# A spectrum held in two layouts in one tile, and its transposes as two row tiles of 64

## The chip, the cores and the metric

The kernel runs on one core of a Trainium2 chip. The metric is the device time of one execution in microseconds; the kernel before takes 2072.28 us in the median of three runs (2070.13 to 2073.51). The lower the better.

## The reference, cut to what matters

```python
# x, v: (4, 11456, 128); pos_emb: (11456, 64); w1: (64, 64); w2: (64, 128)
h = np.maximum(pos_emb @ w1, 0) @ w2 * np.exp(-0.01 * pos)[:, None]
u = x * v
L = 2 * S
y = irfft(rfft(u, n=L, axis=1) * rfft(h, n=L, axis=0), n=L, axis=1)[:, :S]
x = (x * y).reshape(45824, 128)
# then a mixture of 8 experts, top 1
logits = x @ w_gate + modality_bias[modality_id]
e = argmax(logits);  gate = softmax(logits)[e]
out = gate * (relu(x @ w1[e]) @ w2[e])          # F = 1024
```

So there is a long convolution along the sequence, for each of 128 features and four batches, and then a routed feed-forward layer over all rows.

## The kernel before, in words

The convolution is a two-step transform over 90 x 64 indices. The kernel calls the index of the first step k1 (N1 = 90 of them) and the 64 places of the second n2; 128 features d are dealt with in 16 groups q of eight.

One large tile `A` of 128 partitions holds the spectrum between the steps. Its partitions are the 64 places n2 in two halves (one for each of two parts `c`), and its free axis is `[2 blocks, 90 k1, 128 d]`. For each batch it is written twice and read twice:

- `transform` in `forward_stages` (L486 to 499): for a group q, 64 matmuls (each shown as two instructions) multiply the products of x and v with `fwd` (90 columns), and two copies on ACT (L498) write A for four features each, all k1: runs of four neighbouring elements, 512 bytes apart.
- `spectrum` in `middle_stages` (L617): for a step g, that is four values of k1, the moving operand of the matmuls L625 is `A[:, :, k1]`, 256 columns, two runs of 128.
- `inverse` (L657): after the products with the filter's spectrum, matmuls L669 transform back, and two copies on ACT (L673) write the same four k1 of A again, 128 neighbouring features at a time.
- `turn` in `inverse_stages` (L690): for a group q and a block, eight PE transposes (L694) take `A[:, blk, :, d]`, 128 partitions by 90 k1 at a step of 512 bytes, as weights, with the 128 x 128 identity as the moving operand. Four of them fill one PSUM bank, and a copy on ACT (L695) takes each of the two banks to a tile `w_t`. Then `transform` of the inverse (L697) multiplies with `inv` (L703), ACT copies one half of the result (L706), and DVE does the rest (L707 to L709).

The work is laid out in stages: a first stage with the filter and the first batch's products, a middle with 23 steps g, an outer stage, a middle, and so on, and a last outer stage that has only the inverse half. An outer stage has 16 indices q. In it the inverse turns of one batch, the routing of its rows (L751 to L838: the row transposes L751 with copies L753, logits, choice of the expert, storing the rows) and the forward products and transforms of the next batch go side by side. The last stage is followed by the experts (L1079 onwards), which the change does not touch.

The order of all of this is written out by hand: each function is put on a time line with an index and an offset (tables OUTER, LAST, MID0 and MID), the events are sorted, and every engine gets its instructions in that order and keeps it. In OUTER a turn of q comes first, then the row transposes, the forward transform of q - 1, and only then the inverse transform L703 of q. In LAST the inverse transform of q comes right after the second turn of q.

PSUM has four single banks (`bank`, used in rotation by the turns, the inverse's matmuls, the row transposes, the logits and the rest) and two pairs of banks (`pair`, used by the forward transform, the inverse transform and the spectrum). A bank is given back when the copy that reads it is done. Three tiles `xo` hold finished rows until they are stored (L809); L709 writes them.

The choice of experts needs two constant matrices `tri` and `ones`, which come as float32 in `small` and are cast to bfloat16 by DVE (L406).

## Time and profile before

| | |
|---|---|
| median of three runs | 2072.28 us |
| profiled execution | 2074.09 us |
| span of its instructions | 2072.3 us |
| mean granted TensorE clock | 0.982 |
| PE busy | 1958.3 us (94%) |
| DVE busy | 1752.4 us (85%) |
| ACT busy | 1284.4 us (62%) |
| POOL busy | 1169.4 us (56%) |
| transposes of the turns, L694 | 1024, 135.5 us |
| their copies, L695 | 256, 133.5 us |
| spectrum matmuls, L625 | 1440, 181.1 us |
| inverse matmuls, L669 | 3576, 228.1 us |
| forward matmuls, L495 | 4096, 100.1 us |

The span runs from the first to the last instruction of one profiled execution; the execution's own time is what lies around that span too. Busy time counts each moment once, so that overlapping matmuls don't count twice; the mean of one instruction does include such overlap. A releaser is what ended an engine's idle time. The clock is a share of full speed, 2.4 GHz. Up to about 1020 us the kernel is in the convolution and the routing, after that in the experts.

### The profile page before, as it was taken

The numbers are of one execution on the slowest core, as the hardware profiler recorded it, in microseconds if no ns is written. First come the engines' busy times: TensorE is split into PE (matmuls) and PEld (weight loads), VectorE is DVE, ScalarE is ACT, GpSimd is POOL, SyncE is SP. The second block draws the span as 40 slices with busy tenths as digits, with TensorE's granted clock in tenths as the row PEclk, the third lists the DMA queues.
The fourth block names the chain that finished last, engine by engine and source line by source line (L and its number), as shares of the span: only waits on it lengthen the run. The fifth ranks groups of instructions, "written<-read, shape, count | busy, mean of one in ns | idle before, by whom it ended". The sixth has DMA issues, their size and how long they took to land. (4 is left out here: it accounts for less than half of the span.)

```text
span 2072.3 us, 50243 instructions
## 1 busy us (share of the span) xinstructions
PE 1958.3 (94%) x17646; PEld 1554.1 (75%) x17646; DVE 1752.4 (85%) x2612; ACT 1284.4 (62%) x2404; POOL 1169.4 (56%) x1054
## 2 busy tenths in 40 slices
PE   8899898999989998999789999999999999999997
PEld 8688665776667665776468888877888888888897
DVE  6599899999999899996678888897888778878886
ACT  5555675457744675456456666666666666666675
POOL 0144004766678476974456678786555555555654
PEclk9999999999999999999899999999999999999998
DMA  8565688889988898856787456654645555555421
GB/s 319 184 191 173 231 280 268 268 264 314 327 270 253 280 339 288 283 183 179 199 248 205 97 127 138 133 124 103 118 97 97 97 100 98 96 98 100 86 40 29
DMA packets 610842, 379.46 MB, mean 183 GB/s; under 512 B 424026, under 2 KB 542005, under 8 KB 610585
## 3 DMA queue, kind: packets, MB, share of 16 engines
q1 hardware_dynamic: 587193, 328.61, 58.2%
q0 software_dynamic: 23104, 47.34, 6.6%
q8 instruction: 141, 2.31, 0.5%
q14 instruction: 116, 0.95, 0.2%
q10 hardware_dynamic: 288, 0.25, 0.1%
HBM read 272.74 MB, written 103.70 MB: 182 GB/s over the span
## 5 line engine op out<-in xcount | busy, mean ns | idle before, releaser
L1094 ACT ACTIVATE hh<-ph 128x512 fp32r<-128x512 f32 x724 | 434.0, 599 | 323.2 <-PE ph L1091 320.2
L1095 DVE SCALAR_TENSOR_TENSOR hl<-ph,hh 128x512 fp32r<-128x512 f32 x724 | 488.5, 680 | 164.4 <-ACT hh L1094 155.6
L276 POOL DMA_INDIRECT xs<-back,to x360 | 405.4, 1126 | 319.9 <-DVE se L797 107.9
L1160 POOL DMA_INDIRECT out<-ot,x x362 | 373.3, 1031 | 160.2 <-issue 36.7
L1089 PE MATMUL ph<-xh,wh 128*128 128x512 f32 (+1 forms) x792 | 298.0, 376 | 8.3 <-ACT wh L1060 8.3
L1091 PE MATMUL ph<-xl,wh 128*128 128x512 f32 (+1 forms) x792 | 296.2, 374 | 9.0 <-POOL xl L1077 9.0
L1115 PE MATMUL po<-hl,wh 128*128 128x512 f32 (+1 forms) x792 | 295.6, 373 | 0.9 <-DVE hl L1095 0.6
L1090 PE MATMUL ph<-xh,wl 128*128 128x512 f32 (+1 forms) x792 | 295.6, 373 | 0.0
L1113 PE MATMUL po<-hh,wh 128*128 128x512 f32 (+1 forms) x792 | 295.1, 373 | 0.2 <-ACT hh L1094 0.2
L1114 PE MATMUL po<-hh,wl 128*128 128x512 f32 (+1 forms) x792 | 294.7, 372 | 0.0
L673 ACT COPY A<-pw 128x512 f32<-128x512 f32 (+1 forms) x184 | 97.1, 580 | 188.1 <-PE pw L669 188.1
L1077 POOL TENSOR_TENSOR xl<-xT,xh 128x512 fp32r<-128x512 f32 (+1 forms) x77 | 96.2, 1250 | 203.2 <-ACT xh L1073 203.2
L669 PEld LDWEIGHTS pw<-work 64*128 64x128 f32 x2856 | 167.2, 189 | 32.1 <-ACT work L607 19.2
L625 PE MATMUL pz<-A,work 128*64 128x256 f32 x1440 | 181.1, 394 | 8.3 <-DMA work<-in_c_to 5.0
L638 POOL TENSOR_TENSOR work<-work 128x512 f32<-128x512 f32 (+1 forms) x92 | 115.3, 1253 | 129.0 <-DVE work L634 128.4
L669 PE MATMUL pw<-work 64*128 64x128 f32 x2856 | 181.6, 279 | 4.7 <-POOL work L655 4.3
L1091 PEld LDWEIGHTS ph<-xl,wh 128*128 128x128 f32 x792 | 150.5, 190 | 37.0 <-POOL xl L1077 10.8
L1089 PEld LDWEIGHTS ph<-xh,wh 128*128 128x128 f32 x792 | 150.5, 190 | 33.6 <-ACT wh L1060 8.5
L1115 PEld LDWEIGHTS po<-hl,wh 128*128 128x128 f32 x792 | 150.0, 189 | 29.8 <-DVE hl L1095 4.2
L1090 PEld LDWEIGHTS ph<-xh,wl 128*128 128x128 f32 x792 | 150.6, 190 | 26.1 <-DVE wl L1061 0.4
L1113 PEld LDWEIGHTS po<-hh,wh 128*128 128x128 f32 x792 | 150.0, 189 | 26.1 <-ACT hh L1094 0.7
L1114 PEld LDWEIGHTS po<-hh,wl 128*128 128x128 f32 x792 | 150.0, 189 | 25.7
(181 smaller groups left out, 3613.9 us busy)
## 6 DMA issues: line engine op xcount, KB each, us to landing
work<-hs SPq DMA_DIRECT2D x66, 512.0 KB
work<-in_x SPq DMA_DIRECT2D x64, 512.0 KB
work<-in_xd SPq DMA_DIRECT2D x58, 512.0 KB
work<-in_v SPq DMA_DIRECT2D x51, 512.0 KB
xr<-xo SPq DMA_DIRECT2D x64, 365.6 KB
back<-xr SPq DMA_DIRECT2D x120, 195.0 KB
work<-in_c_to SPq DMA_DIRECT2D x88, 256.0 KB
blocks<-xs SPq DMA_DIRECT2D x328, 64.0 KB
```

Source lines behind the costliest of these rows:

```text
L276: s = pool.indirect_dma_start(out=xs, out_offset=bass.IndirectOffsetOnAxis(ap=ix, axis=0), in_=src, in_offset=None, bounds_check=E * R - 1 ...
L625: pe.matmul(z[64 * s:64 * s + 64, t, r], k["b"][:, t, s, r], A[:, :, 4 * g + 2 * t + s], start=True, stop=True)
L669: pe.matmul(v[s][:, t, blk], k[of][at, t, r, blk], k["c"][at, t, r], start=i == 0, stop=i == len(terms) - 1)
L1089: pe.matmul(p, k[0, "h"][:, f:f + D], k["xh"], start=True, stop=False)
L1090: pe.matmul(p, k[0, "l"][:, f:f + D], k["xh"], start=False, stop=False)
L1091: pe.matmul(p, k[0, "h"][:, f:f + D], k["xl"], start=False, stop=True)
L1094: act.activation(hh, ph, AF.Relu)
L1095: steps.append(ins_of(dve.scalar_tensor_tensor(hl, ph, 0.0, hh.bitcast(F32), op0=ALU.max, op1=ALU.subtract)))
L1113: pe.matmul(po, k[1, "h"][:, f], hh[:, t], start=g == 0, stop=False)
L1114: pe.matmul(po, k[1, "l"][:, f], hh[:, t], start=False, stop=False)
L1115: pe.matmul(po, k[1, "h"][:, f], hl[:, t], start=False, stop=g == NCH - 1)
L1160: s = pool.indirect_dma_start(out=out, out_offset=bass.IndirectOffsetOnAxis(ap=ix, axis=0), in_=src, in_offset=None, bounds_check=N - 1, o ...
```

## The change

The tile A is laid out anew, as `[32 groups, 736]`, where a group is a block and eight features, and the 90 k1 are padded to KP = 92. Two views of the same words are used in turn. `A_fwd` has in each group first k1 mod 4, then k1 div 4, then the eight features: the forward copies write fours of features, 32 bytes apart, and the spectrum reads 32 rows of eight. `A_inv` has in each group four pairs, and for each pair all k1 with the two features of the pair side by side: the inverse's copies write pairs, and the turns read 90 k1 at a step of 8 bytes. A step g of the middle reads and writes the same words in both views.

A turn is now 16 transposes instead of eight: each takes 64 partitions and a 64 x 64 part of the identity, and the two halves of the partitions go to two banks `p[0]` and `p[1]`. Both banks are taken at the start, and each of the two copies takes one bank, that is one half of the rows for all eight features, to blocks of 64 in `w_t`.

`fwd` has 92 columns, two of them zero. The matrices `tri` and `ones` come as bfloat16 inside `small`, so the cast goes. The tiles mx, mb and se of the choice have one buffer instead of two.

```diff
@@ -37,6 +37,7 @@
 N = B * S
 NP = N1 // 2
 NM = (NP + 1) // 2
+KP = 4 * NM
 NQ = N2 // 4
 NO = N2 // 8
 NC = 16
@@ -98,8 +99,8 @@
     turn = 2 * np.pi / (8 * N1)
     phi = turn * (((4 * k1[None, :] + 1) * (2 * n1[:, None] + 1)) % (8 * N1))
     even, odd = np.cos(phi) + np.sin(phi), np.cos(phi) - np.sin(phi)
-    fwd = np.zeros((2, 64, 2, N1))
-    fwd[:, :HALF, 0], fwd[:, :HALF, 1] = even, odd
+    fwd = np.zeros((2, 64, 2, KP))
+    fwd[:, :HALF, 0, :N1], fwd[:, :HALF, 1, :N1] = even, odd
     whole = np.zeros((2, 64, 2, N1))
     whole[:, :HALF, 0], whole[0, :HALF, 1], whole[1, :HALF, 1] = even, odd, -odd
     inv = np.zeros((N1, 2, 64))
@@ -131,7 +132,8 @@
     keep = np.ones((D, E, NC))
     keep[:, :, 0] = 0
     q, p = np.arange(D)[:, None], np.arange(D)[None, :]
-    tri = np.concatenate([-(q >= p).astype(float), np.ones((D, D))], 1)
+    tri = np.concatenate([-(q >= p).astype(np.float32), np.ones((D, D), np.float32)], 1)
+    tri = np.ascontiguousarray(tri.view(np.uint32) >> 16).astype(np.uint16).view(np.float32)
     small = np.concatenate([
         order(tok)[:, 0:NC],
         first.reshape(D, E * NC), keep.reshape(D, E * NC), tri,
@@ -142,7 +144,7 @@
     pad[:, :, D + 1] = np.array(NOWHERE, np.int32).view(np.float32)
     f = lambda a: np.ascontiguousarray(a, dtype=np.float32)
     return {
-        "c_fwd": f(fwd.reshape(D, 2 * N1)), 
+        "c_fwd": f(fwd.reshape(D, 2 * KP)), 
         "c_inv": f(inv.reshape(N1, D)), "c_to": f(to), "c_back": f(back), "c_early": f(np.concatenate([win.reshape(D, 2 * N2), whole.reshape(D, 2 * N1)], 1)),
         "c_small": f(small), "c_pad": f(pad.reshape(D, -1)),
     }
@@ -173,7 +175,7 @@
 SMALL = {}
 _at = 0
 for _name, _n in (("tok", NC), ("first", E * NC), ("keep", E * NC),
-                  ("tri", D), ("ones", D), ("reg", E), ("iota", NF)):
+                  ("both", D), ("reg", E), ("iota", NF)):
     SMALL[_name] = (_at, _at + _n)
     _at += _n
 NSMALL = _at
@@ -212,7 +214,7 @@
     warm = cst.tile([1, 2], F32, name="warm")
     dve.memset(warm, 0.0)
 
-    both = cst.tile([D, 2 * D], BF16, name="both")
+    both = sm("both").bitcast(BF16)
     tri, ones = both[:, 0:D], both[:, D:2 * D]
     base = cst.tile([D, E], F32, name="base")
     base1 = cst.tile([D, E], F32, name="base1")
@@ -375,8 +377,10 @@
             return pairs.tile([D, 2, 512], F32, tag="pp", name=name)
 
         work = keepp.tile([D, 17 * U + 4 * PU], F32, name="work")
-        A = keepp.tile([D, 2, N1, D], F32, name="A")
-        fwd = keepp.tile([D, 2, N1], F32, name="fwd")
+        A = keepp.tile([D, 2 * NQ, 8 * KP], F32, name="A")
+        A_fwd = A.rearrange("p (b q) (j g n) -> p b q j g n", b=2, j=4, n=8)
+        A_inv = A.rearrange("p (b q) (h k i) -> p b (q h) k i", b=2, h=4, i=2)
+        fwd = keepp.tile([D, 2, KP], F32, name="fwd")
         inv = keepp.tile([N1, 2, 64], F32, name="inv")
         bs2 = keepp.tile([D, NO, E, NC], F32, name="bs2")
         early = bs2.rearrange("p o e c -> p (o e c)")[:, 0:2 * N2 + 2 * N1]
@@ -403,7 +407,6 @@
 
         def split_constants():
             dve.tensor_scalar_add(base, sm("reg"), FAR)
-            dve.tensor_copy(both, small[:, SMALL["tri"][0]:SMALL["ones"][1]])
 
         pool.memset(wg, 0.0)
 
@@ -420,7 +423,7 @@
 
         flat = lambda t: t.rearrange("p a b c r -> p (a b c r)")
         spans = back.rearrange("p k c r -> p (k c r)")
-        flatA = A.rearrange("p b k d -> p (b k d)")
+        flatA = A.rearrange("p c r -> p (c r)")
         for name, of in (
                 ("emb", [flatA[:, (16 + i) * U // 2:(17 + i) * U // 2] for i in range(NQ)]),
                 ("c0", [spans[:, i * U // 2:(i + 1) * U // 2] for i in range(3)]),
@@ -492,11 +495,10 @@
                         for c in range(2):
                             for blk in range(2):
                                 at = slice(64 * blk, 64 * blk + 64)
-                                pe.matmul(p[64 * c:64 * c + 64, blk, N1 * j:N1 * j + N1],
+                                pe.matmul(p[64 * c:64 * c + 64, blk, KP * j:KP * j + KP],
                                           e[at, c, 4 * h + j], fwd[at, c], start=True, stop=True)
-                    d0 = 8 * q + 4 * h
-                    act.copy(A[:, :, :, d0:d0 + 4],
-                             p[:, :, 0:4 * N1].rearrange("p b (n k) -> p b k n", n=4))
+                    act.copy(A_fwd[:, :, q, :, :, 4 * h:4 * h + 4],
+                             p[:, :, 0:4 * KP].rearrange("p b (n g j) -> p b j g n", n=4, j=4))
 
             return load, product, transform
 
@@ -623,7 +625,7 @@
                     for r in range(2):
                         for s in range(2):
                             pe.matmul(z[64 * s:64 * s + 64, t, r], k["b"][:, t, s, r],
-                                      A[:, :, 4 * g + 2 * t + s], start=True, stop=True)
+                                      A_fwd[:, :, :, 2 * t + s, g], start=True, stop=True)
                 k["pz"] = pz[:, 0:n].rearrange("p t (r b d) -> p (t r) b d", r=2, b=2)
 
             def products(g):
@@ -670,8 +672,8 @@
                                           start=i == 0, stop=i == len(terms) - 1)
                 for s in range(2):
                     k1 = 4 * g + s
-                    act.copy(A[:, :, k1:k1 + 2 * n - 1:2].rearrange("p b t m -> p t b m"),
-                             v[s][:, 0:n])
+                    act.copy(A_inv[:, :, :, k1:k1 + 2 * n - 1:2].rearrange("p b m t i -> p t (b m) i"),
+                             v[s][:, 0:n].rearrange("p t b (m i) -> p t (b m) i", i=2))
 
             todo = dict(inverse=inverse, spectrum=spectrum, products=products, load_c=load_c,
                         load=load, swap=swap)
@@ -688,11 +690,15 @@
                 sp.dma_start(t, a["x"][b, q])
 
             def turn(q, blk):
+                p = [bank("wt")[0:N1].rearrange("p (c j n) -> p c j n", c=2, j=4) for _ in range(2)]
                 for c in range(2):
-                    p = bank("wt")
                     for j in range(4):
-                        pe.transpose(p[0:N1, D * j:D * j + D], A[:, blk, :, 8 * q + 2 * j + c], ident)
-                    act.copy(w_t[q % 2][blk][:, c], p[0:N1])
+                        for t in range(2):
+                            at = slice(64 * t, 64 * t + 64)
+                            pe.transpose(p[t][:, c, j], A_inv[at, blk, 4 * q + j, 0:N1, c], ident[at, at])
+                w = w_t[q % 2][blk].rearrange("p c (j t n) -> p t c j n", j=4, t=2)
+                for t in range(2):
+                    act.copy(w[:, t], p[t])
 
             def transform(q):
 
@@ -776,7 +782,7 @@
                 i = b * NO + o
                 xo = xo_of(b, o)
                 lg = kept.pop(o)
-                mx = rt.tile([PU, NC], F32, tag="mx", name="mx")
+                mx = rt.tile([PU, NC], F32, tag="mx", name="mx", bufs=1)
                 dve.tensor_reduce(mx, ec(lg), axis=AX.X, op=ALU.max)
                 dl = lg
                 dve.tensor_sub(dl, lg, wide(mx))
@@ -785,14 +791,14 @@
                 oh, sc = oh_t[i % 2], sc_t[i % 2]
                 sco = rt.tile([PU, E, NC], F32, tag="sco", name="sco", bufs=1)
                 dve.scalar_tensor_tensor(sco, dl, 0.0, fst, op0=ALU.is_ge, op1=ALU.mult)
-                mb = rt.tile([PU, NC], F32, tag="mb", name="mb")
+                mb = rt.tile([PU, NC], F32, tag="mb", name="mb", bufs=1)
                 dve.tensor_reduce(mb, ec(sco), axis=AX.X, op=ALU.max)
                 dve.scalar_tensor_tensor(oh[0:PU], sco, 0.5, wide(mb), op0=ALU.max,
                                          op1=ALU.is_equal)
                 dve.tensor_tensor_scan(
                     sc[0:PU].rearrange("p e c -> p (e c)"), sm("keep")[0:PU],
                     oh[0:PU].rearrange("p e c -> p (e c)"), 0.0, op0=ALU.mult, op1=ALU.add)
-                se = rt.tile([PU, NC], F32, tag="se", name="se")
+                se = rt.tile([PU, NC], F32, tag="se", name="se", bufs=1)
                 dve.tensor_reduce(se, ec(ex), axis=AX.X, op=ALU.add)
                 dve.tensor_scalar_add(se, se, 1e-9)
                 xov = xo[0:PU].rearrange("p w s h r -> p h (w s) r")
```

## Rows read from the trace of the kernel before

**Rows 1.** the page's part 1: busy us (share of the span) xinstructions

```profile
PE 1958.3 (94%) x17646; PEld 1554.1 (75%) x17646; DVE 1752.4 (85%) x2612; ACT 1284.4 (62%) x2404; POOL 1169.4 (56%) x1054
```

**Rows 2.** stretches: us; busy of PE, PEld, DVE, ACT, POOL; clock, DMA, GB/s

```profile
96.00:208.00 112.00, 111.44 (x1388) 91.17 (x1384) 102.08 (x98) 63.20 (x132) 49.15 (x39) 1.00 0.57 180
240.00:330.00 90.00, 86.84 (x1325) 59.97 (x1324) 85.16 (x157) 68.69 (x134) 3.31 (x4) 1.00 0.78 265
```

**Rows 3.** timeline of PE, 228 to 241 us: start, us, engine, line, operation

```profile
230.49 1.94 PE L703 MATMUL py<-work,inv 90*64 90x512 f32 x8
...
232.35 2.01 PE L694 MATMUL wt<-ident,A 128*90 128x128 f32 x16
...
236.77 1.94 PE L703 MATMUL py<-work,inv 90*64 90x512 f32 x8 [0.26 <-ACT A L498]
```

**Rows 4.** timeline of ACT, 230 to 241 us

```profile
232.47 0.59 ACT L706 COPY work<-py 128x512 f32<-128x512 f32 x1 [1.10 <-PE py L703]
233.14 2.06 ACT L695 COPY work<-wt 90x512 f32<-90x512 f32 x4
...
235.96 1.42 ACT L498 COPY A<-s 128x720 f32<-128x720 f32 x2
```

**Rows 5.** waits of DVE, 225 to 800 us: total us, times, longest

```profile
DVE work L707 <- ACT work L706: 18.2, 16, 3.2
```

**Rows 6.** timeline of PE, 916 to 945 us

```profile
922.50 2.00 PE L694 MATMUL wt<-ident,A 128*90 128x128 f32 x16
924.43 2.36 PE L703 MATMUL py<-work,inv 90*64 90x512 f32 x8
926.72 1.14 PE L694 MATMUL wt<-ident,A 128*90 128x128 f32 x8
```

**Rows 7.** timeline of ACT, 916 to 945 us

```profile
923.23 2.06 ACT L695 COPY work<-wt 90x512 f32<-90x512 f32 x4
```

**Rows 8.** timeline of DVE, 984 to 1012 us

```profile
988.45 0.25 DVE L802 RECIPROCAL xo<-se 109x16 f32<-109x16 f32 x1
...
997.09 1.23 DVE L709 TENSOR_TENSOR xo<-work 128x1024 f32<-128x1024 f32 x1 [2.82 <-DMA xr<-xo]
```

**Rows 9.** groups by line and form: xcount, busy us, mean ns, idle before

```profile
L669 PE MATMUL pw<-work 64*128 64x128 f32 x2856 | 181.6, 279 | 4.7 <-POOL work L655 4.3 <-DVE work L655 0.3
...
L625 PE MATMUL pz<-A,work 128*64 128x256 f32 x1440 | 181.1, 394 | 8.3 <-DMA work<-in_c_to 5.0 <-DVE work L643 2.3 <-ACT A L498 0.9
...
L694 PE MATMUL wt<-ident,A 128*90 128x128 f32 x1024 | 135.5, 283 | 2.9 <-ACT A L673 2.9
L695 ACT COPY work<-wt 90x512 f32<-90x512 f32 x256 | 133.5, 600 | 10.3 <-PE wt L694 7.1 <-ACT work L761 0.2 <-issue 0.2
...
L673 ACT COPY A<-pw 128x512 f32<-128x512 f32 x176 | 94.5, 589 | 185.2 <-PE pw L669 185.2
...
L498 ACT COPY A<-s 128x720 f32<-128x720 f32 x128 | 92.0, 762 | 21.5 <-PE s L495 20.8
...
L495 PE MATMUL s<-fwd,work 64*64 64x90 f32 x3264 | 77.6, 242 | 6.1 <-DVE work L708 4.1 <-issue 1.5 <-ACT A L498 0.4
...
L526 ACT ACTIVATE A<-m,bs 128x64 f32<-128x64 f32 x32 | 7.2, 387 | 13.1 <-PE m L515 13.1
...
L673 ACT COPY A<-pw 128x256 f32<-128x256 f32 x8 | 2.6, 375 | 2.8 <-PE pw L669 2.8
```

**Rows 10.** lines L495, L669, L694, weight loads: ns min/median/max, first and last start

```profile
L495 PEld LDWEIGHTS s<-fwd,work x3264: 129/133/223, 60.3 to 798.0; 64*64 64x64 f32 x192
...
L669 PEld LDWEIGHTS pw<-work x2856: 182/188/334, 351.4 to 917.1; 64*128 64x128 f32 x191
...
L694 PEld LDWEIGHTS wt<-ident,A x1024: 177/180/216, 220.9 to 1007.7; 128*90 128x90 f32 x171
```

**Rows 11.** timeline of all engines, 587 to 600 us

```profile
592.11 1.95 PE L625 MATMUL pz<-A,work 128*64 128x256 f32 x16
...
593.98 2.95 PE L669 MATMUL pw<-work 64*128 64x128 f32 x48
```

## The prediction, made before the changed kernel was run

> **What bounds the kernel now.** The first part of the page [rows 1] is read first: PE is busy 94% of the span, DVE 85%, ACT 62%. From that alone any PE time that is taken away would seem to be time won. The next view is the table of stretches [rows 2], because the change touches only the outer stages and the four middles between them, and these have different limits. The middle of the first row leaves PE 0.56 us of 112 idle: there a slower matmul costs its full time. The outer stage of 240 to 330 us has PE at 86.84 of 90 and DVE at 85.16 of 90, both nearly full, so that the busy shares don't tell which of them ends a step.
>
> So the chain inside an outer stage has to be followed. Early in each stage it is this [rows 3, 4]: L703 starts on PE at 230.49, its result is copied by ACT (L706) at 232.47, then ACT runs the four copies of the turns (L695, from 233.14), two of the rows' turn and the first spectrum copy (L498, 235.96), and L703 of the next index starts at 236.77, when that copy has given back its pair of banks (the mark "0.26 <-ACT A L498"). The steps are 1.98 + 0.67 + 2.82 + 0.81 = 6.28 us, the whole period. The loop goes over ACT, which has no idle mark from L706 on, and PE has 0.26 us to spare in it. Later in the stage DVE sets the pace: in 225 to 800 us, three outer stages and the two middles between them, it waited for L706 16 times and 18.2 us in all [rows 5]. That 18.2 us is the most that a faster turn can give back there.
>
> The last stage has two phases. First it is paced by the turn, its copies and L703, 926.72 - 922.50 = 4.2 us per index until other work joins it [rows 6]. Towards its end a loop without PE sets the pace [rows 8]: the choice ends with L802 at 988.45, its rows are stored, and the next L709 has waited 2.82 us for such a store when it starts at 997.09.
>
> **The change part by part.**
>
> *Turn, on PE.* A turn is now 8 transposes of 128 rows; after, 16 of 64 rows with 64 streamed columns, in two row tiles. Two turns take 924.43 - 922.50 = 1.93 us from start to start [rows 6], so one takes 0.965 us. No row shows a transpose in two row tiles. The nearest is L669, 64 rows in two row tiles with 128 weight columns and 128 streamed ones: 181.6 us for 2856, 63.6 ns each [rows 9]. Taken whole it gives 16 x 63.6 = 1.02 us, 0.05 more than now; scaled by streamed columns (64/128) 0.51 us, 0.46 less. I take it scaled by weight columns (90/128): 45 ns, 0.72 us, 0.25 less, because with only 64 streamed columns the load should be the longer part. Over 128 turns that is 31 us of PE work less (7 more to 58 less).
>
> *Turn, on ACT.* The same two copies of 512 elements (600 ns [rows 9]), but each now holds one half of the rows for all eight indices, so both wait for the end of the turn. Today the first copy starts 923.23 - 922.50 = 0.73 us after the turn begins [rows 6, 7]: 0.48 us for four transposes and 0.25 us on the way. After the change it starts at 15/16 of 0.72 + 0.25 = 0.93 us. In the loop of rows 3 and 4 the copies begin 233.14 - 232.35 = 0.79 us after the turn does, so the loop grows by 0.14 us although PE does less. About ten indices of the three stages are in that phase (16 waits, some of them in the phase that DVE sets): +1.4 us. What PE saves there becomes idle time before L703.
>
> *Last stage.* L703's second matmul reads the second block, and now needs both copies of it instead of the first alone. Four copies take 2.06 us [rows 7]; the last ends at 922.50 + 0.93 + 2.06 = 925.49. L703 then has three quarters of its 1.86 us (232.35 - 230.49) to go and ends at 926.9 against 926.72 if its two column tiles overlap again at once, at 927.2 if the first of the three runs alone. I take +0.35 us; six indices before the store's loop takes over: +2.0 us. In that loop a turn that is a few tenths later costs nothing; without slack the other ten indices would cost 3.5 us more, which I keep for the range, as I keep zero for the first six.
>
> *Forward transform.* 92 streamed columns for 90. The largest group of L495 has 3264 instructions in 77.6 us [rows 9], so all 4096 (64 per index) make 97 us; 2.2% is 2.1 us of PE, of which a quarter, the first stage's share, lies on the path: +0.5 us. Its copy has 736 elements instead of 720: 13 ns at the rate that L498 and L673 show between them, (762 - 589)/208 = 0.83 ns per element, inside the rounding of the 1.4.
>
> *Inverse's copies (L673).* They write runs of two elements instead of 128. Runs of four cost nothing: L498 already writes fours, and L673's 375 ns for 256 and 589 for 512 put 720 at 763; it took 762. Single elements do cost something: L526, 64 of them at a step of 256 bytes, took 387 ns where the same line gives 215; 2.7 ns for each, unless its scale operand has a part in it [rows 9]. So pairs lie between 0 and 256 x 1.67 = 427 ns more per copy, the upper end if a run of two takes as long as a run of four. I take 0, since the nearest row with runs is free. The upper end is a rival below. The Trainium skill's "SBUF — State Buffer" (SBUF: two separate sides, on cachelines of 16 bytes) says that two hits on a line are enough for full bandwidth; by it the pairs are free and the sum stays, and the upper end would add the rival's 12 us. No run here shows it for ACT.
>
> *Spectrum's reads (L625).* 256 columns in 32 rows of eight instead of two of 128. No moving operand of this size in the trace has steps. The nearest row is a weight load of this same tile: 90 columns at 512 bytes took 180 ns, where 64 and 128 adjacent ones took 133 and 188, so 155 for 90 [rows 10]: 25 ns for 90 hops, 0.28 ns per hop. For 32 hops in one instruction that is 9 ns, for 1440 instructions 13 us; nothing below zero, since these reads are contiguous now. I take 0: seven of eight reads stay adjacent.
>
> *The rest.* One DVE cast goes, estimated from the small DVE operations around L802 (0.25 us [rows 8]) at -0.3 us. The tiles mx, mb and se keep one buffer; DVE alone writes and reads them, in order, so nothing waits. No DMA is added or moved past another on SP's or POOL's queue.
>
> Sum: +1.4 + 2.0 + 0.5 - 0.3 = +3.6 us. The profiled execution took 2074.09 us with a span of 2072.3, 1.8 us above the median of the runs, 2072.28; the difference is put on the median: 2075.9 us. 0.2%, 4.1 us, is about what a measurement of this kernel can tell from no change, so this is a forecast of no measurable change that leans to slower.
>
> **The rivals.**
>
> *The turn is on the path after all.* DVE's 16 waits in the outer stages [rows 5] end with the ACT copy behind L703, PE is 96% busy there [rows 2], and the last stage has six indices that the turn paces. If the ACT copies pack closer than I think, each of the 22 shrinks by what a turn saves on PE, 22 x 0.25 to 22 x 0.46, 5.5 to 10 us. Against it stands ACT's loop without a gap [rows 4]. Time: 2064.
>
> *Slower, the reads of rows of eight.* In the middles PE runs L625 and L669 back to back (592.11 + 1.87 = 593.98 [rows 11]), so every ns per L625 is paid. At the 9 ns above: 13 us, 2085. It decides from 3 ns per instruction (4.1 us / 1440). For it: strided weights do load slower. Against: seven of eight reads stay adjacent.
>
> *Slower, pairs on ACT.* At 427 ns the two copies of a step take 0.85 us longer, and the swap's copies behind them, for which DVE waits in the first middle, come later. ACT is busy 63.20 us of 112 there [rows 2], so I let half of it through: 23 steps x 0.43 make 10 us; the other middles add 2: 2084.
>
> *The middle loses its overlap.* Both layouts lie over the same words. If a step's spectrum had to wait for the copies of an earlier step's inverse, PE would stand for two copies of 589 ns and the 0.25 us on the way, 1.4 us in each of 92 steps, 130 us. For it: the patterns of all steps interleave through the whole tile. Against it: a step reads and writes the same words, other steps others, and today's patterns interleave too without such a wait in the group's row of L625 [rows 9]. 2206 at worst.
>
> **How the numbers follow.** Forecast 0.48 (own range 2072 to 2080), turn on the path 0.27, reads 0.10, pairs 0.10, overlap lost 0.05. Faster by over 0.2%: 0.26 of the second and 0.02 of the first, 0.28. Slower: 0.14 of the first and 0.24 of the last three, 0.38. The same: the rest, 0.34. The range 2062 to 2092 takes in the second case (5.5 to 10 us), the bounds of reads and pairs, and leaves out lost overlap and reads at several times 9 ns.
>
> **What would show it.** L694 should have 2048 instructions and less busy time than its 135.5 us, with L625's mean still near 394 ns and L673's near 589. The loop of rows 4 should be 0.1 to 0.2 us longer with more idle time before L703, and the waits of L707 for L706 as long as now or longer. Wrong: L694's group above 150 us, L625 above 400 ns, L673 above 650 ns, L707's waits down by over 5 us, or a wait of L625 for L673.

## The result, and the profile after

The changed kernel takes 2099.49 us in the median of four runs (2092.9 to 2101.9), the kernel before 2072.78 us beside it: a ratio of 1.0132, 95% interval 1.0118 to 1.0146, so 1.3% slower. 2075.9 us had been forecast, 24 us less, and the measured time lies outside the range. The profiled execution took 2099.63 us with a span of 2097.9.

The first part of the page after, against [rows 1]:

```profile
PE 1962.9 (94%) x18670; PEld 1531.0 (73%) x18670; DVE 1750.9 (83%) x2611; ACT 1301.9 (62%) x2404; POOL 1156.5 (55%) x1054
```

The groups of the lines that the change touches (busy us, mean ns, idle time before), against [rows 9]. L698, L701, L627, L675 and L500 are the former L694, L695, L625, L673 and L498:

```profile
L627 PE MATMUL pz<-A,work 128*64 128x256 f32 x1440 | 182.3, 396 | 8.8 <-DVE work L645 5.6 <-DMA work<-in_c_to 1.2 <-DVE work L636 1.1
...
L701 ACT COPY work<-wt 90x512 f32<-90x512 f32 x256 | 145.5, 582 | 35.4 <-PE wt L698 31.3
...
L698 PE MATMUL wt<-ident,A 64*90 64x64 f32 x2048 | 111.4, 249 | 13.8 <-ACT work L701 9.1 <-ACT A L675 3.0
...
L675 ACT COPY A<-pw 128x512 f32<-128x512 f32 x176 | 103.8, 650 | 179.9 <-PE pw L671 179.9
...
L500 ACT COPY A<-s 128x736 f32<-128x736 f32 x128 | 94.1, 782 | 18.9 <-PE s L498 18.4 <-DMA xo<-in_v 0.2
```

The transposes did get shorter: 111.4 us for 135.5. The spectrum's reads of rows of eight cost nothing (396 ns for 394). The writes of pairs cost 61 ns each (650 for 589). And ACT is now idle for 35.4 us before the turns' copies, where it was 10.3.

The middles did not move (first to last spectrum matmul 126.3, 106.1, 104.0 and 108.4 us before; 127.0, 103.7, 106.3 and 108.4 after). The time went into the stages with turns. From the first to the last L713 (the former L707) the three outer stages take 108.2, 108.1 and 108.2 us for 103.0, 104.0 and 105.6, and the last stage 101.0 for 90.2: 5.2 + 4.1 + 2.6 + 10.8 = 22.7 of the 25.6 us by which the span grew. The rest lies ahead of the first turn (1.9) and in the experts (1.7), about what these parts differ by between kernels that share their code: the first L713 came between 226.9 and 231.7 us in the runs below.

**An outer stage.** PE of the kernel before, in its first outer stage, over one whole period of two indices. One of them has the logits (L759) and is called the long index here, the other the short one:

```profile
258.80 0.94 PE L759 MATMUL pl<-work,wg 128*32 128x436 f32 x8
...
264.95 1.94 PE L703 MATMUL py<-work,inv 90*64 90x512 f32 x8 [0.26 <-ACT A L498]
266.82 2.00 PE L694 MATMUL wt<-ident,A 128*90 128x128 f32 x16
268.66 0.91 PE L751 MATMUL xT<-ident,xo 109*128 109x109 f32 x8
269.51 1.49 PE L495 MATMUL s<-fwd,work 64*64 64x90 f32 x64
271.24 1.94 PE L703 MATMUL py<-work,inv 90*64 90x512 f32 x8 [0.23 <-ACT A L498]
273.10 0.94 PE L759 MATMUL pl<-work,wg 128*32 128x436 f32 x8
```

and of the changed kernel, the same stretch of work:

```profile
261.93 0.94 PE L765 MATMUL pl<-work,wg 128*32 128x436 f32 x8
...
263.03 0.97 PE L698 MATMUL wt<-ident,A 64*90 64x64 f32 x17
264.58 0.89 PE L698 MATMUL wt<-ident,A 64*90 64x64 f32 x15 [0.59 <-ACT work L701]
...
268.52 1.94 PE L709 MATMUL py<-work,inv 90*64 90x512 f32 x8 [0.26 <-ACT A L500]
270.39 1.56 PE L698 MATMUL wt<-ident,A 64*90 64x64 f32 x32
271.94 1.21 PE L757 MATMUL xT<-ident,xo 109*128 109x109 f32 x8
273.08 1.50 PE L498 MATMUL s<-fwd,work 64*64 64x92 f32 x64
275.17 1.94 PE L709 MATMUL py<-work,inv 90*64 90x512 f32 x8 [0.59 <-ACT A L500]
277.04 0.94 PE L765 MATMUL pl<-work,wg 128*32 128x436 f32 x8
```

The period was 273.10 - 258.80 = 14.30 us and is 277.04 - 261.93 = 15.11. In the kernel before PE has only two small gaps (0.26 and 0.23) in it, both for ACT's copy: the loop of PE and ACT was itself 14.3 us long. DVE's loop was level with it. In the next period of the kernel before, where DVE has no idle mark at all, its L707 stands

```profile
273.84 0.70 DVE L707 TENSOR_TENSOR work<-py,work 128x512 f32<-128x512 f32 x1
...
288.15 0.69 DVE L707 TENSOR_TENSOR work<-py,work 128x512 f32<-128x512 f32 x1
```

that is 14.31 us from one to the next but one. The short index grew from 271.24 - 264.95 = 6.29 to 275.17 - 268.52 = 6.65 us, although its two turns shrank from 1.84 to 1.55: L757 takes 0.3 longer and L709 waits 0.59 for 0.23. The long one, the rest of the period, grew from 8.01 to 8.46: its second turn stops after one transpose and waits 0.59 us for a bank, because a turn now takes both of its banks at once.

ACT of the changed kernel in the short index, against [rows 4]:

```profile
270.51 0.59 ACT L712 COPY work<-py 128x512 f32<-128x512 f32 x1 [0.43 <-PE py L709]
271.31 2.29 ACT L701 COPY work<-wt 90x512 f32<-90x512 f32 x4 [0.21 <-PE wt L698]
273.50 0.94 ACT L759 COPY work<-xT 128x436 f32<-128x436 f32 x2
274.33 1.47 ACT L500 COPY A<-s 128x736 f32<-128x736 f32 x2
```

1.99 + 0.80 + 3.02 + 0.84 = 6.65 us. The second term grew by 0.13 (0.67 before): the copies start late, 0.92 us after the turn. The third grew by 0.20 (2.82 before): four copies take 2.29 us for 2.06. Both copies of a turn write interleaved blocks of 64 in one region of `w_t`, and the second carries a wait for the first, which it did not have.

DVE's waits, of the changed kernel from 225 to 810 us, against [rows 5], then in the last stage (920 to 1020 us):

```profile
DVE work L713 <- ACT work L712: 32.7, 27, 2.3
...
DVE work L713 <- ACT work L712: 25.4, 13, 3.9
DVE ro L831 <- PE pr L829: 4.9, 4, 1.2
```

The kernel before in its last stage (920 to 1020 us):

```profile
DVE work L707 <- ACT work L706: 12.3, 10, 2.7
DVE xo L709 <- DMA xr<-xo: 12.2, 5, 3.0
```

**The last stage.** The waits for stores are gone, and those for ACT have doubled: the loop over the turns paces the whole stage. Its PE, against [rows 6], first at the start, then at two later indices:

```profile
930.78 1.56 PE L698 MATMUL wt<-ident,A 64*90 64x64 f32 x32 [0.76 <-ACT A L675]
932.96 3.03 PE L709 MATMUL py<-work,inv 90*64 90x512 f32 x8 [0.61 <-ACT work L701]
935.91 1.56 PE L698 MATMUL wt<-ident,A 64*90 64x64 f32 x32
...
1016.48 0.88 PE L698 MATMUL wt<-ident,A 64*90 64x64 f32 x16
...
1019.88 1.07 PE L709 MATMUL py<-work,inv 90*64 90x512 f32 x2
1021.16 1.93 PE L709 MATMUL py<-work,inv 90*64 90x512 f32 x6 [0.21 <-ACT work L701]
...
1030.43 0.88 PE L698 MATMUL wt<-ident,A 64*90 64x64 f32 x16
```

An index is 935.91 - 930.78 = 5.13 us instead of 4.22, and a later pair 1030.43 - 1016.48 = 13.95 us, where L707 came 8.63 + 4.25 = 12.88 us apart in the kernel before. In LAST the inverse matmul follows the second turn at once, so that PE stands while ACT copies (the marks of 0.61 and 0.21).

### The profile page after: what moved, and what is told of

Its sections match the earlier page's. It is cut to its first block, busy times and chain, and to the rows that moved or that the text cites. A ratio compares the mean times of both kernels' runs of the same rounds, so it can differ in the third digit from the quotient of the medians.

```text
span 2097.9 us, 52014 instructions
## 1 busy us (share of the span) xinstructions
PE 1962.9 (94%) x18670; PEld 1531.0 (73%) x18670; DVE 1750.9 (83%) x2611; ACT 1301.9 (62%) x2404; POOL 1156.5 (55%) x1054
## 5 line engine op out<-in xcount | busy, mean ns | idle before, releaser
L278 POOL DMA_INDIRECT xs<-back,to x360 | 392.9, 1091 | 358.0 <-DVE sc L798 112.0
L675 ACT COPY A<-pw 128x512 f32<-128x512 f32 (+1 forms) x184 | 106.5, 639 | 181.6 <-PE pw L671 181.6
L627 PE MATMUL pz<-A,work 128*64 128x256 f32 x1440 | 182.3, 396 | 8.8 <-DVE work L645 5.6
L1120 PEld LDWEIGHTS po<-hh,wl 128*128 128x128 f32 x792 | 149.9, 189 | 25.6
```

The source lines that it names most:

```text
L278: s = pool.indirect_dma_start(out=xs, out_offset=bass.IndirectOffsetOnAxis(ap=ix, axis=0), in_=src, in_offset=None, bounds_check=E * R - 1 ...
L627: pe.matmul(z[64 * s:64 * s + 64, t, r], k["b"][:, t, s, r], A_fwd[:, :, :, 2 * t + s, g], start=True, stop=True)
L1120: pe.matmul(po, k[1, "l"][:, f], hh[:, t], start=False, stop=False)
```

## Experiments

Four kernels at a time ran beside the kernel before, on four chips. Chip 1: the layout, the turn, late copies, halves in runs of 64. Chip 2: the change again, the second copy's wait, halves in runs of 256, the new LAST. Chip 3: the other orders. Chip 4: the change once more and the three that mix the turns. The kernel before took 2111 us on chips 1 and 2, 2070 and 2072 on 3 and 4. So ratios are compared, and beside them the spacing of L713 in the first outer stage, which was the same to 0.01 us in all three profiles of the change (9.13 + 5.98 = 15.11 a pair). The length of a whole stage is compared only between kernels on chips of the same kind: on chip 1 the outers of the layout alone, which is level with the kernel before, took 109.0, 111.9 and 113.3 us.

**The layout with the old turn.** The turn of the kernel before, from `A_inv`:

```diff
-                        for t in range(2):
-                            at = slice(64 * t, 64 * t + 64)
-                            pe.transpose(p[t][:, c, j], A_inv[at, blk, 4 * q + j, 0:N1, c], ident[at, at])
...
+                        pe.transpose(p[0:N1, D * j:D * j + D], A_inv[:, blk, 4 * q + j, 0:N1, c], ident)
+                    act.copy(w_t[q % 2][blk][:, c], p[0:N1])
```

> The changed kernel with the turn of before: eight transposes of 128 rows, one bank and one copy for each parity of the feature, read from the new layout at a step of 8 bytes. Theory (the turn's way to its copies costs the 27 us: both copies begin only after the whole turn and come 0.57 to 0.60 us apart instead of 0.48): about 2075 us, that is before plus the 1.7 us by which the first stage grew; the copies of the turn are 0.48 us apart and the last stage takes 111 us from its first turn to the experts' first matmul, as before, not 122.7. Rival A (the layout costs: pair writes of 650 ns for 589, first copies of 782 for 762, 92 columns): 2094 to 2100, since nothing of that is undone.

Measured 1.0015 (0.9997 to 1.0034), pairs of 14.30 us. The layout, and with it the 92 columns of `fwd`, the constants and the tiles with one buffer, costs nothing that can be told, although the inverse's copies took 650 ns here too. It even shortens the weight load of a turn:

```profile
L696 PE MATMUL wt<-ident,A 128*90 128x128 f32 x1024 | 131.9, 279 | 5.4 <-ACT A L675 3.0 <-issue 2.2
L696 PEld LDWEIGHTS wt<-ident,A 128*90 128x90 f32 x1024 | 114.4, 163 | 44.2 <-issue 25.3 <-PE py L705 7.3 <-DVE sco L789 4.1
```

163 ns a load in the mean at a step of 8 bytes; at 512 the mean was 183 (median 180, [rows 10]).

**The turn with the old layout.**

```diff
-                        pe.transpose(p[0:N1, D * j:D * j + D], A[:, blk, :, 8 * q + 2 * j + c], ident)
...
+                        for t in range(2):
+                            at = slice(64 * t, 64 * t + 64)
+                            pe.transpose(p[t][:, c, j], A[at, blk, :, 8 * q + 2 * j + c], ident[at, at])
...
```

> The kernel before with the new turn alone: 16 transposes of 64 rows in two row tiles, read from the old layout at a step of 512 bytes. Theory: 2094 to 2099 us, with copies of the turn 0.57 to 0.60 us apart, the loop of an outer stage at 6.6 us for 6.28 and the last stage at 122 us. Rival A (the layout): 2072 to 2076. Besides: if the step of the weights matters for row tiles, two turns take clearly more than the 1.55 us of the changed kernel; else the same.

Measured 1.0188 (1.0154 to 1.0221), pairs of 9.39 + 6.17 = 15.56 us. The turn alone carries the loss. Without the layout it gains nothing on PE:

```profile
L696 PE MATMUL wt<-ident,A 64*90 64x64 f32 x2048 | 131.6, 269 | 17.5 <-ACT work L699 8.5 <-issue 4.0 <-ACT A L673 3.3
L696 PEld LDWEIGHTS wt<-ident,A 64*90 64x90 f32 x2048 | 116.8, 209 | 61.1 <-issue 34.3 <-ACT work L699 11.6 <-DVE mb L793 5.7
```

**Late copies alone.** The kernel before, its transposes of 128 rows filling both banks in turn, so that both copies start late and neither waits for the other:

```diff
+    p = [bank("wt") for _ in range(2)]
+    for j in range(4):
+        for c in range(2):
+            pe.transpose(p[c][0:N1, D * j:D * j + D], A[:, blk, :, 8 * q + 2 * j + c], ident)
```

> The kernel before, with the eight transposes of a turn in another order: the two parities alternate, so that both banks are full only at the end and both copies start late, as in the changed kernel, but 128 rows, old layout, copies 0.48 us apart. First copy at 7/8 of 0.965 + 0.25 = 1.09 us after the turn's start, later than the changed kernel's 0.92. If the late start alone makes the cost: 2090 us or more. If, as I think, the closer pace of the copies keeps the outer stages under DVE's 14.3 us for two indices (6.28 + 0.3 and some 7.3 + 0.3 us), only the last stage and the first indices pay: 2076 to 2082.

Measured 1.0089 (1.0060 to 1.0119), more than the 4 to 10 us expected; pairs of 9.16 + 6.31 = 15.47 us. Late copies and two banks at once are enough to lengthen the pair by more than the change does (15.11), without row tiles and without a wait between copies. The copies here start even later than the change's, 1.12 us after the turn for 0.92, so the run shows what such a delay does and not how much of the change's loss it is. In the last stage the delay costs 7.0 us (96.5, and 89.5 with the layout alone on the same chip), less than the change's 10.8. The late start and the taking of both banks are not told apart by any run; what each does is read from the traces alone.

**The second copy's wait alone.** The kernel before, a bank holding both `c` of two pairs of indices: copies as early as before, but to interleaved parts of `w_t`:

```diff
+    for h in range(2):
+        p = bank("wt")[0:N1].rearrange("p (c r) -> p c r", c=2)
...
+        act.copy(w_t[q % 2][blk][:, :, 2 * D * h:2 * D * h + 2 * D], p)
```

> The kernel before, with its turns of 128 rows and its early copies, but a bank holds both c of two index pairs, so that the two copies of a turn write to interleaved parts of w_t and the second waits for the first; nothing else. Theory (the wait costs only where the loop has no slack): copies come 0.57 instead of 0.48 us apart, the loop of two indices grows by 0.4 to about 14.0 us and stays under DVE's 14.3, the last stage grows by about 3: ratio 1.0015 (1.000 to 1.003). Rival (the wait is the main cost of the change): 1.008 or more.

Measured 1.0039 (1.0021 to 1.0057), over what I expected. On PE:

```profile
264.63 1.94 PE L705 MATMUL py<-work,inv 90*64 90x512 f32 x8 [0.26 <-ACT A L498]
...
271.12 1.94 PE L705 MATMUL py<-work,inv 90*64 90x512 f32 x8 [0.47 <-ACT A L498]
```

The short index is 6.49 us for 6.29, 0.20 us more; four copies take 2.33 us here for 2.06. The pair is 9.17 + 5.56 = 14.73. The slack of 0.3 us that I still supposed is not there; a longer loop lengthens the pair at once.

**The change without that wait.** First with each copy in a half of its own and the inverse matmul reading runs of 64, then with runs of 256 and the order put right in L712 to L714:

```diff
-    act.copy(w[:, t], p[t])
+    act.copy(w_t[q % 2][blk][:, t], p[t].rearrange("p c j n -> p (c j n)"))
...
+    w_t[q % 2][blk].rearrange("p t (c r) -> p c t r", c=2)[:, c]   # 2nd version; 1st: "p t (c j n) -> p c j t n"
```

> The changed kernel, but each half's copy goes to 512 words of its own instead of every other block of 64, and the inverse matmuls read the two halves in rows of 64; the second copy then need not wait for the first to finish. Theory: the four copies of an index come 0.48 us apart, 0.2 to 0.3 us sooner in all, the outer loop falls from 6.65 to about 6.4 us and two indices to below DVE's 14.3, which gives back 8 to 10 us there and some 4 us in the last stage: about 2086 us. Rival B (the late start and the two banks at once are all of it, the pace of the copies nothing): 2096 to 2100.

> The changed kernel, but each copy of a turn fills a half of w_t of its own (row tile t, then c, j, n), the inverse matmul reads two runs of 256, and the order of columns is put right in the ACT copy and the two DVE additions behind it (runs of 64). The second copy no longer overlaps the first's region. Theory (late start and the second copy's wait for the first together push the PE and ACT loop past DVE's 14.3 us for two indices): four copies in 2.06 us instead of 2.29, the short index of an outer stage from 6.65 to about 6.45 us, two indices from 14.33 to about 13.9, which DVE then covers, so the three outers lose most of their 3 to 4 us each, and the last stage about 3 of its 11: ratio 1.007 (1.004 to 1.009). Rival (the late start alone does it, the wait is free): 1.013 as the change. Rival (the wait alone does it): 1.000 to 1.003. Runs of 64 on DVE could cost: then its additions take over 0.69 us.

> The changed kernel once more, unaltered, as the measure for the runs beside it. Every theory expects its first ratio to the kernel before, 1.013 (1.012 to 1.015).

Measured 1.0228 (1.0187 to 1.0269) and 1.0217 (1.0196 to 1.0238). The change itself, beside the second of them, gave 1.0227 (1.0176 to 1.0279) instead of the 1.013 I expected: no gain could be seen there, and one under 0.5% could not have been. The reads in runs of 64 were not to blame: eight inverse matmuls still took 1.94 us in the first outer stage. PE in the second version:

```profile
265.81 1.94 PE L708 MATMUL py<-work,inv 90*64 90x512 f32 x8 [0.26 <-ACT A L500]
...
272.27 1.94 PE L708 MATMUL py<-work,inv 90*64 90x512 f32 x8 [0.47 <-ACT A L500]
```

and its ACT, in the second outer stage:

```profile
476.21 2.04 ACT L700 COPY work<-wt 90x512 f32<-90x512 f32 x4 [0.27 <-PE wt L698]
```

Four copies in 2.04 us, the short index at 6.46. But the long index still waits for a bank (0.64 us), and the pair is 14.97 for 15.11. I had taken DVE to cover all above that; it does not.

What made the change lose 1% more on these chips sits mainly in the last stage. Against the layout alone on chip 1, the change's outers on chip 2 (112.2, 117.1 and 118.1 us) are 13.2 us longer in sum, close to the 11.9 of the first comparison; but its last stage of 115.0 us is 25.5 longer, where the first comparison gave 10.8. In it the granted clock fell (it is the third column from the end; the last row lies mostly at the lower of the two levels, 1.2 GHz):

```profile
980.00:1000.00 20.00, 17.83 (x155) 9.42 (x153) 11.73 (x23) 11.42 (x23) 6.80 (x7) 1.00 0.46 133
1000.00:1020.00 20.00, 19.82 (x129) 9.74 (x126) 9.49 (x24) 8.75 (x19) 5.82 (x6) 0.58 0.61 158
```

Two inverse transforms (L709) in that stretch took 4.59 and 4.93 us on PE, where they take about 3.0 at the full clock. Ahead of it PE stood for copies at every index (17.83 us busy of 20). In the first profile of the change, with the clock at 1.00 from 960 to 1040 us, the stage took 101.0. The clock fell in the last stage of both runs of halves as well (118.5 and 117.9 us), but not with the turn in the old layout on chip 1 (107.6 us), where PE waits too. Why it fell there and not elsewhere stays open.

**Where the loss sits.** The old turn in the last stage alone, and in the outers alone:

```diff
+    turn = turn_128 if b == nb - 1 else turn_64      # outers only; the other run has them exchanged
```

> The changed kernel, unaltered, as the whole to which the two halves beside it are added: 1.013 on a chip where the kernel before takes some 2072 us, 1.023 where it takes some 2111.

> The changed kernel, with the turns of 128 rows and early copies in the last stage alone; the three outer stages keep the two row tiles. Theory (two places of loss that add: 5 us in each outer, by 0.8 us a pair of indices, and 11 us in the last stage): the last stage is that of before, the outers those of the change: ratio 1.007 (1.005 to 1.009) on the faster kind of chip. Rival (it is one loss, and stages downstream pass it on): near 1.013 or near 1.000.

> The reverse: row tiles in the last stage alone, turns of 128 rows and early copies in the outers. Theory: pairs of 14.3 us in the outers, the last stage 101 us as in the change: ratio 1.006 (1.004 to 1.008); its excess and that of the run with row tiles in the outers alone add to the change's within 0.002.

Measured 1.0118 (1.0093 to 1.0144) for the change, 1.0064 (1.0044 to 1.0085) for the outers alone, 1.0051 (1.0035 to 1.0068) for the last stage alone: 0.64% + 0.51% = 1.15%. Two losses that add. The spacing says the same: 108.2, 108.2, 108.2 and 89.8 us with row tiles in the outers; 103.5, 103.6, 104.6 and 101.0 with them in the last stage.

**The order of the stages.** In the last stage both turns behind the inverse, in the outers the row transposes behind the forward transform:

```diff
-LAST = ("inverse:1 logits:3 turn0:0 half:2 lturn:3 turn1:0 ...
+LAST = ("inverse:1 turn0:0 turn1:0 logits:3 half:2 lturn:3 ...
...
-OUTER = ("turn0:0 turn1:0 lturn:3 biased:3 half:2 product:0 forward:1 ...
+OUTER = ("turn0:0 turn1:0 lturn:3 biased:3 product:0 forward:1 half:2 ...
```

> The changed kernel, with the order of the last stage's table altered alone: inverse, turn0, turn1, logits, half, lturn instead of inverse, logits, turn0, half, lturn, turn1, so that a turn's copies are not followed at once by the matmuls that read them. Theory (in the last stage the copies stand bare between the second turn and the inverse matmul, 0.6 us of wait at each index and more): the stage falls from 101.8 us to 88 to 93, the kernel to 1.007 (1.005 to 1.009) of before, 9 to 13 us under the change. Rival (the last stage is paced by its stores or by the routing's DVE chain, and the copies only show there): no change, 1.013. Rival (the logits then come late and lturn waits): up to 1.016.

> The changed kernel with the outer stages' table altered alone: half (the transposes of rows and their copies on ACT) behind forward instead of ahead of it. Theory (the late copies push the row copies and the forward copies of ACT back, and the inverse matmul waits 0.6 us for a buffer that the first forward copy has to empty): the forward copy now stands 0.95 us earlier on ACT, that wait goes, the pair of indices in the first outer falls from 15.11 us to 14.3 to 14.6, some 8 to 15 us less over three outers: ratio 1.006 to 1.010 on a chip where the change is 1.013, 1.015 to 1.020 where it is 1.023. Rival (the time is in the turns themselves, the second of which waits for a bank): pairs stay at 15.1, no change. The last stage stays as in the change under both.

> The changed kernel with both orders: half behind forward in the outers, and in the last stage both turns behind the inverse, ahead of logits and half. Theory: both places of the loss are closed, the outers at DVE's 14.3 to 14.6 a pair, the last stage as before: ratio 1.002 (0.999 to 1.006). Rival (the late start costs in any order): 1.008 or more.

> As the run with both orders, and the two copies of a turn in separate halves of w_t, so that the second does not wait for the first (copies 0.48 us apart again). Theory: 0.1 us a turn less on ACT, worth something only if ACT still paces: ratio 0 to 0.002 under the run with both orders, 1.001 (0.998 to 1.005); under 1.000 it would beat the kernel before. Rival: the same as with both orders.

> The kernel before with the same two orders, nothing of the change. Theory (its outers are paced by DVE's 14.30 us a pair and its last stage by DVE and the stores, so that the order of PE and ACT is free): 1.000 (0.998 to 1.003). Rival (the orders are better in themselves): 0.995 or less; then what the orders win in the changed kernel is no mending of the change.

> Row tiles in the last stage alone, and there with both turns behind the inverse, ahead of logits and half. Theory (both places of loss closed, one by the old turn and one by the order; PE paces neither stage): 1.000 (0.998 to 1.003). Rival (PE's 0.2 us a turn is worth something where the last stage is busiest on PE): 0.998 or less, and this version would beat both.

Measured: LAST alone 1.0115 (1.0097 to 1.0134) beside a change of 1.0227, its last stage 92.3 us for 115.0 (part of that is the clock above; on chip 3, with it at 1.00 in both down to the stage's end, the new LAST made 91.9 of 101.0). OUTER alone 1.0090 (1.0056 to 1.0125); pairs of 9.13 + 5.79 = 14.92 us, not the 14.3 to 14.6 expected. Both 1.0064 (1.0047 to 1.0082), both with separate halves 1.0045 (1.0028 to 1.0062), not told apart from each other; outers of 105.2 to 105.9 us, last stages of 91.9 and 90.5. The kernel before with both orders 1.0026 (1.0012 to 1.0039). Row tiles in the last stage alone, with the new LAST, 1.0014 (0.9999 to 1.0029).

The new LAST gives back nearly all of the last stage (91.9 us, and 90.2 in the kernel before). There the stores are waited for again; DVE's waits with both orders, from 925 to 1010 us:

```profile
DVE work L713 <- ACT work L712: 15.0, 9, 2.7
DVE xo L715 <- DMA xr<-xo: 8.6, 4, 2.5
```

The new OUTER frees L709 from its wait but has one of its own. PE of the run with it alone:

```profile
268.63 0.86 PE L498 MATMUL s<-fwd,work 64*64 64x92 f32 x32
270.21 0.86 PE L498 MATMUL s<-fwd,work 64*64 64x92 f32 x32 [0.71 <-DVE work L714]
...
271.90 1.94 PE L709 MATMUL py<-work,inv 90*64 90x512 f32 x8
```

The forward's second pair of banks is the one that DVE reads the last inverse from. So the order has a floor of 14.92 to 15.0 us whatever the turn is; the kernel before rises to 9.21 + 5.78 with it. In the profiled executions the outers with this order take 106.1 to 106.4 us without row tiles, so that in it row tiles no longer lengthen them. No version here is faster than the kernel before.

## Why the prediction was wrong, point by point

- *Turn, on PE*: right. Two turns take 1.55 us from start to start, 48 ns a transpose (45 forecast), 24 us of busy time less (31 forecast). Scaling by weight columns fits: between the two layouts the row tiles' group and its mean weight load change by the same factor (131.6/111.4 = 209/177 = 1.18). For 128 rows they do not (135.5/131.9 = 1.03, 183/163 = 1.12).
- *Turn, on ACT*: this is the step that failed, in its size and in its count. The first copy comes 0.92 us after the turn (0.93 forecast), and that part of the loop grew by the 0.13 expected (0.14). But "the same two copies" left out that the second waits for the first when they write interleaved blocks: 0.20 us more an index (shown by the run with that alone, 6.49 us, and by the run without it, 6.46). And taking two banks at once stops the second turn of the long index for 0.59 us, which no step had. That wait is read from the trace; no run has it without late copies. A short index costs 0.36 us instead of 0.14, a long one 0.45.
- *Its count* was the larger part. "About ten indices" rested on DVE setting the pace later in the stage. DVE did run there without a gap (14.31 us a pair), but the other loop was 14.30 us long as well: its short index, 6.28 us, stood in [rows 3, 4], and the long one was never added up. With no slack every pair pays 0.81 us. That gives 5.2 us in the first outer stage and 11.9 in all three, where 1.4 was forecast. The rival "the turn is on the path after all" had the path right and the sign wrong.
- *Last stage*: the term of 2.0 us measures 10.8. Each early index costs 0.9 us instead of 0.35: L709 not only lacks the second block's copies, PE stands 0.61 us before it and 0.67 within it (3.03 for 2.36). And the loop of stores, which was to absorb the rest after six indices, was hardly the longer one: 12.88 us a pair against 13.95 now. "The other ten indices would cost 3.5 us more" was the right worry with too small a price. Shown by the run with row tiles there alone (101.0 us, 0.5% in all) and by the new LAST in that run (93.5 us, 0.1%).
- *Forward transform* (+0.5) and *the DVE cast* (-0.3) are too small to be told from what the first part differs by between runs.
- *Inverse's copies*: +61 ns, near the lower end of 0 to 427, and hidden: the layout alone measures 1.0015 with it. The Trainium skill's "SBUF — State Buffer" (SBUF: two separate sides, on cachelines) would have made pairs free; the measurement differs and decides.
- *Spectrum's reads*: right, 396 ns for 394. *Overlap lost*: did not happen.
- The range held the costs of the middle, which turned out free, and no case in which the outers' loop had no slack. The Trainium skill's "TensorEngine Tiling (Array Packing)" (PSUM Bottleneck) warns that after a fourfold speedup of TensorE by tiling the copies out of PSUM may become the bottleneck. The trace agrees in that the copies stand on the path, but ACT was busy only 11.16 of the 15.11 us of a pair: what cost time was when the copies could start and what waited for them, not their rate.

## What to carry to other kernels

Before an engine without gaps is called the bound, add up every other loop over a whole period, start to start, long and short index together: here the second was 14.30 us as well, and a delay that looked free lengthened every pair. When a producer fills two banks at once, ask when the first consumer can start, whether the two consumers still write separate regions, and who else needs the banks; time taken off the producer is worth nothing if its consumers start later. Where a consumer's reader follows on the producer's own engine, put other work of that engine between them (the last stage took 91.9 us instead of 101.0 here).

## What the runs showed of the hardware

- A transpose of 64 rows by 90 columns with 64 streamed took 48 ns in two row tiles with weights at a step of 8 bytes. Its weight load took 177 ns, against 209 at 512 bytes, where the whole group took 131.6 us instead of 111.4. With 128 rows: 163 against 183, and the group 131.9 us against 135.5.
- ACT copies of 582 to 600 ns follow each other every 0.49 us ((2.06 - 0.60) / 3) when they are independent, and every 0.57 when the second of two waits for the first.
- A moving operand of 256 columns in rows of eight reads as fast as one of two runs of 128 (396 and 394 ns); an ACT copy of 512 columns that writes pairs of elements takes 10% longer (650 for 589 ns).
- The same change cost 1.2 to 1.3% where the kernel before takes some 2072 us and 2.3% where it takes 2111; there the granted clock fell to 0.58 in the last stage.
